# Layer norm in chunks of two tiles with flips amid the matmuls, a convolution spread over the weight gradients, and pinned weight pieces in a fused backward kernel

## The chip, the cores and the metric

The kernel runs on one core of a Trainium2 chip. The metric is the device time of one execution in microseconds (us), lower is better. All inputs and outputs are bfloat16. Executions of one kernel scatter by some 3 to 5 us to either side of their median, so a difference of a few us between two kernels is only told from several runs of both on the same chip, and a difference of 2 us between two single traces is not told at all.

## The reference, cut to what matters

The reference is the forward value and all gradients of a sum of two branches on a layer-normalised input:

```python
xn  = layernorm(x)                                   # x: [2048, 1024]
A   = xn * (causal_conv(shift(k) * v) + D * shift(k) * v)      # long convolution
B   = (relu(xn @ W_gate) * (xn @ W_up)) @ W_down     # W_gate, W_up: [1024, 3584]
out = x + A + B
# returned: out, and the gradients of x, k, v, shift_k, ssm_k, ssm_D, W_gate, W_up, W_down
```

The MLP branch B has the large matrix products. The convolution of branch A is done with transforms written as small matmuls, of which the copies out of PSUM go to ScalarE and VectorE.

## The kernel before

The matrix work of B comes in four phases, and the convolution's steps are woven into the first and second ones:

1. **First phase** (`hidden`): gate, up and hidden gradient, for 2 halves of 8 row tiles and 7 blocks of 512 columns. At its very start the layer norm runs in chunks, and TensorE "flips" (transposes) each normalised tile into `xnT`.
2. **Weight gradients** (`grad_down`, `grad_in`).
3. **Output phase** (`out_phase`): `h @ W_down`, for 16 row tiles. Beside it, the weights of the last phase are loaded transposed.
4. **Last phase** (`grad_x`): the gradient of x, and a tail after the last matmul.

The start and the loop of the first phase (cut):

```python
LN_CHUNKS = (1, 1, 2, 4, 4, 4)
self.e1 = tc.alloc_tile_pool(name="b_e1", bufs=3, side="left")  # ht AND gh live in these 3 buffers
...
def gate_up(sp):
    while len(xT) < sp + 2:                 # flips of both tiles, just before they are used
        while len(self.xn) <= len(xT):
            next(ln)                        # one more chunk of layer norm
        xT.append(self.flip_xn(len(xT)))
    ...
    for s in (sp, sp + 1):                  # up, and the store of h
        self.gemm8(ps, xT[s], wu)
        ht = self.e1_tile("ht")
        ...
        nc.sync.dma_start(out=h_d[...], in_=ht[:])
def grad(sp):
    for s in (sp, sp + 1):
        self.gemm8(ps, gT[s], wd)           # ps_h
        gh = self.e1_tile("gh")
        nc.scalar.copy(out=gh[:], in_=ps[:])
        ...
```

The mixing of the two branches: each piece of MLP work tells its nominal length, and that length times the pace is what the convolution has to wait for its next step. A lower pace makes the convolution slower.

```python
A_START = 55_000                            # ns of MLP work before the convolution starts
yield 0.9, b.hidden(...)
yield 1.3, b.grad_down(...)
yield 1.3, b.grad_in(...)
```

The output phase and the tail (cut):

```python
for st in range(16):
    hT = self.tall(h_d, st, "hT")                             # transposed load, SyncE
    nc.sync.dma_start(out=ya[:], in_=y_d[rows, :])
    nc.sync.dma_start(out=xe[:], in_=xn_d[rows, :])
    nc.sync.dma_start(out=xr[:], in_=x[rows, :])
    if st < 8:                                                # 8 pieces of 256 rows
        nc.sync.dma_start_transpose(out=wT[:, :, c:c + 256], in_=w[c:c + 256, :])
    nc.vector.tensor_tensor(out=ya[:], in0=ya[:], in1=xe[:], op=ALU.mult)
    nc.vector.tensor_tensor(out=ya[:], in0=ya[:], in1=xr[:], op=ALU.add)
    ...                                                       # 56 matmuls; o0 = ps + ya; store o0
# tail of the last phase, per row tile
V.tensor_scalar(out=gm[:], in0=gt[:], scalar1=m[:, 4:5], scalar2=None, op0=ALU.add)
for ob in range(2):
    V.scalar_tensor_tensor(out=gx[:, oc], in0=xn[:, oc], scalar=m[:, 7:8], in1=gx[:, oc], ...)
    V.scalar_tensor_tensor(out=o1[:, oc], in0=gx[:, oc], scalar=rstd, in1=gm[:, oc], ...)
```

The order of instructions on an engine comes from a priority that each instruction gets when it is traced (`pri.now()`, `pri.late()`). `keep_in_program_order` pins an instruction behind what was traced before it on its engine.

## Time and profile before

| | before |
|---|---|
| median of the first three runs | 2003.51 us (1997.66 to 2004.28) |
| profiled execution (span) | 1995.9 us |
| first phase: first matmul of the weight gradients starts at | 712.7 us |
| weight gradients | 688.2 us |
| output phase | 199.5 us |
| last phase | 386.6 us |
| after the start of the last matmul | 8.8 us |

The phases are read from the timeline of TensorE: each begins with the first matmul into its own PSUM tile (`ps_d`, `ps_o`, `ps_x`). Their lengths add up to the span. (The prediction's 8.4 us for the tail counts from the end of the last matmul.) Two of TensorE's waits (engine, line, tile, what it waited for, us in total, times, longest):

```profile
PE ps_g L599 <- DVE xnT L625: 13.0, 4, 7.6
PE ps_o L799 <- DMA hT<-h_d: 5.6, 3, 2.8
```

These are the two that the change is mainly aimed at: 13.0 us for flipped tiles at the start, 5.6 us for `hT` in the output phase.

### The profile page before, as it was taken

To read this page: it belongs to the slowest core of one execution; us is meant where nothing else is said; L and a number is where in the kernel's file an instruction comes from. 1 tells how busy PE (TensorE), PEld (TensorE's weight loads), DVE (VectorE), ACT (ScalarE), POOL (GpSimd) and SP (SyncE) were. 2 spreads that over 40 slices of the span, in tenths; PEclk is the share of its full clock that TensorE was granted. 3 is DMA by queue.
4 is the path that set the end of the run, shared out by engine and by line. 5 is a ranking of instruction groups with operands and counts; after the bars stand their busy time and mean duration, and the time that the engine had idled before them with its cause. 6 is when DMAs were issued, how large, how long until landed. Compare 5 with 4: busy or idle time off the path is not lost.

```text
span 1995.9 us, 27044 instructions
## 1 busy us (share of the span) xinstructions
PE 1929.1 (97%) x10817; PEld 914.2 (46%) x11022; DVE 995.7 (50%) x1460; ACT 693.8 (35%) x912; POOL 15.5 (1%) x36
## 2 busy tenths in 40 slices
PE   5999999999999999999999999999999999999998
PEld 2445445445444444444454444444444444444443
DVE  4879679679677747666685650000122222333322
ACT  5665365456446428484564741111000000000000
POOL 1000000000000000000000000000000000000000
PEclk9999999999999999999999999999999999999999
DMA  9864676974674774444645359432999555445551
GB/s 280 219 167 130 168 190 159 219 191 124 170 184 127 199 208 126 121 136 131 197 145 138 110 157 316 148 97 67 224 264 231 137 124 120 120 119 125 125 125 40
DMA packets 614895, 318.32 MB, mean 159 GB/s; under 512 B 449896, under 2 KB 584048, under 8 KB 614768
## 3 DMA queue, kind: packets, MB, share of 16 engines
q1 hardware_dynamic: 613488, 312.38, 59.7%
q0 software_dynamic: 1280, 4.20, 0.6%
q8 instruction: 86, 1.41, 0.3%
q14 instruction: 41, 0.34, 0.1%
HBM read 141.36 MB, written 95.44 MB: 119 GB/s over the span
## 4 chain that ended last, share of the span: by engine, by line
PE 46%; ACT 2%; SPq 1%; DMA 1%; issue 1%; DVE 0%; DVEq 0%
PE ps_x L832 19%; PE ps_w L715 17%; PE ps_o L799 8%; PE ps L65 1%; SPq L791 1%; DMA hT<-h_d 1%; ACT G L69 1%; ACT H L69 0%; SPq L768 0%; ACT K L69 0%; ACT wi L753 0%; DMA out_dram<-wi 0%; ACT B L69 0%; PE pst L280 0%; SPq L785 0%
## 5 line engine op out<-in xcount | busy, mean ns | idle before, releaser
L715 PE MATMUL ps_w<-ugs,xn_nat 128*128 128x512 bf16 x1746 | 395.3, 379 | 3.3 <-issue 1.0
L599 PEld LDWEIGHTS <-xnT 128*128 128x128 bf16 x1792 | 169.7, 99 | 217.5 <-issue 23.8
L715 PEld LDWEIGHTS <-xn_nat 128*128 128x128 bf16 x1792 | 170.9, 98 | 203.3 <-issue 8.4
L599 PE MATMUL ps_g<-wg,xnT 128*128 128x512 bf16 x869 | 211.3, 388 | 18.9 <-DVE xnT L625 13.0
L715 PE MATMUL ps_d<-g_nat,hs 128*128 128x512 bf16 x867 | 205.1, 381 | 4.4 <-DMA hs<-h_d 2.5
L599 PE MATMUL ps_h<-wdT,goT 128*128 128x512 bf16 x875 | 205.1, 379 | 1.4 <-issue 0.3
L599 PE MATMUL ps_u<-wu,xnT 128*128 128x512 bf16 x868 | 204.2, 379 | 1.5 <-issue 0.3
L799 PE MATMUL ps_o<-wd,hT 128*128 128x512 bf16 x878 | 193.1, 379 | 6.6 <-DMA hT<-h_d 5.6
L832 PE MATMUL ps_x<-wuT,guT 128*128 128x512 bf16 x878 | 197.5, 379 | 1.0
L832 PE MATMUL ps_x<-wgT,ggT 128*128 128x512 bf16 x878 | 197.3, 379 | 0.9
L801 DVE TENSOR_TENSOR o<-ps_o,ya 128x512 bf16<-128x512 f32 x32 | 21.5, 688 | 272.5 <-PE ps_o L799 272.5
L753 ACT CAST wi<-ps_w 128x512 bf16<-128x512 f32 x112 | 65.5, 586 | 233.4 <-PE ps_w L715 225.0
L799 PEld LDWEIGHTS <-hT 128*128 128x128 bf16 x896 | 87.4, 98 | 112.1 <-DMA hT<-h_d 7.1
L832 PEld LDWEIGHTS <-ggT 128*128 128x128 bf16 x896 | 87.7, 98 | 105.7
L832 PEld LDWEIGHTS <-guT 128*128 128x128 bf16 x896 | 87.7, 98 | 105.7
L834 DVE CUSTOM_DVE_ANT_0 gx<-ps_x,gy 128x512 f32<-128x512 f32 x32 | 22.1, 691 | 226.2 <-PE ps_x L832 215.5
L672 ACT CAST gh<-ps_h 128x512 bf16<-128x512 f32 x112 | 65.5, 585 | 190.1 <-PE ps_h L599 108.3
L599 PEld LDWEIGHTS <-goT 128*128 128x128 bf16 x896 | 84.1, 98 | 97.8 <-issue 6.1
L715 PEld LDWEIGHTS <-hs 128*128 128x128 bf16 x896 | 82.7, 98 | 100.7 <-issue 10.0
L291 DVE STREAM_TRANSPOSE flp<-B 128x1024 f32<-128x1024 f32 x48 | 90.2, 1934 | 47.1 <-ACT B L69 46.7
L69 ACT CAST C<-ps 128x1024 bf16<-128x1024 f32 x96 | 96.8, 1017 | 47.4 <-PE ps L65 47.4
L660 DVE SCALAR_TENSOR_TENSOR ru<-ru,ps_u 128x512 bf16<-128x512 bf16 x112 | 76.3, 681 | 71.0 <-PE ps_u L599 55.2
(156 smaller groups left out, 1711.0 us busy)
## 6 DMA issues: line engine op xcount, KB each, us to landing
ug_d<-ru SPq DMA_DIRECT2D x112, 256.0 KB, 3.1
ugs<-ug_d SPq DMA_DIRECT2D x112, 256.0 KB, 4.4
wg<-in_B_W_gate_dram SPq DMA_DIRECT2D x56, 256.0 KB, 5.0
wu<-in_B_W_up_dram SPq DMA_DIRECT2D x56, 256.0 KB, 3.2
h_d<-ht SPq DMA_DIRECT2D x112, 128.0 KB, 1.9
hs<-h_d SPq DMA_DIRECT2D x56, 256.0 KB, 4.4
out_dram<-wi SPq DMA_DIRECT2D x56, 256.0 KB, 2.2
gt<-in_grad_out_dram SPq DMA_DIRECT2D x32, 256.0 KB, 3.9
```

The source lines that it names most:

```text
L65: self.nc.tensor.matmul(out, lhsT=lhsT, rhs=rhs, start=start, stop=stop)
L69: self.nc.scalar.copy(out=out, in_=in_)
L291: self.nc.vector.transpose(out=df[:, c0:c0 + 32, :], in_=sf[:, c0:c0 + 32, :])
L599: self.nc.tensor.matmul(ps[:], lhsT=xT[:, kt * P:(kt + 1) * P], rhs=w(kt), start=(kt == 0), stop=(kt == self.DT - 1))
L660: nc.vector.scalar_tensor_tensor(out=ru[s][:, 1, :], in0=ru[s][:, 0, :], scalar=0.0, in1=ps[:], op0=ALU.is_gt, op1=ALU.mult)
L672: nc.scalar.copy(out=gh[:], in_=ps[:])
L715: self.nc.tensor.matmul(ps[:], lhsT=lhsT(st), rhs=rhs(st), start=(st == 0), stop=(st == self.ST - 1))
L753: nc.scalar.copy(out=wo[:, d, :], in_=ps[:])
L799: nc.tensor.matmul(ps[:], lhsT=hT[:, kt, :], rhs=self.wd[:, kt, oc], start=(kt == 0), stop=(kt == self.FT - 1))
L801: nc.vector.tensor_tensor(out=o0[:, oc], in0=ps[:], in1=ya[:, oc], op=ALU.add)
L832: nc.tensor.matmul(ps[:], lhsT=T[:, kt, :], rhs=W[:, kt, oc], start=(i == 0), stop=(i == n - 1))
L834: V.tensor_tensor_reduce(out=gx[:, oc], in0=ps[:], in1=gy[:, oc], scale=1.0, scalar=0.0, op0=ALU.add, op1=ALU.add, accum_out=m[:, ob:ob + 1])
```

## The change

The intent has four parts. **A**: the flips of later tiles are traced between the matmuls of earlier ones, so that TensorE has work while VectorE copies them, and the layer norm goes in smaller chunks. **B**: the convolution gets pace 1.0 in the weight gradients. **C**: the last phase's weights are loaded in 16 pieces of 128 rows, one per row tile, each pinned. **D**: a step of the tail moves to ScalarE. The diff, cut to its core:

```diff
-    LN_CHUNKS = (1, 1, 2, 4, 4, 4)
+    LN_CHUNKS = (1, 1, 2, 2, 2, 4, 4)
...
+            if i == 2:
+                self.tc.keep_in_program_order(mean)
...
-                    if ahead:
-                        next(ln, None)
...          # in grad(sp):
+                        if ahead and s == sp + 1:
+                            flip(min(sp + 6, HS))
                         ps = self.ps_tile("ps_h")
...          # the first block
                 if ahead:
+                    flip(2)
+                    next(ln)
                     yield from gate_up(0)
+                    next(ln)
+                    yield from gate_up(2)
+                    next(ln)
                 for sp in range(0, HS, 2):
...
                     yield from grad(sp)
+                    if ahead and sp + 4 < HS:
+                        next(ln, None)
+                        yield from gate_up(sp + 4)
...          # output phase
-            if st < 8:
-                w, wT = (Wg, self.wgT) if st < 4 else (Wu, self.wuT)
-                c = (st % 4) * 256
-                nc.sync.dma_start_transpose(out=wT[:, :, c:c + 256], in_=w[c:c + 256, :])
+            w, wT = (Wg, self.wgT) if st < 8 else (Wu, self.wuT)
+            c = (st % 8) * P
+            tc.keep_in_program_order(nc.sync.dma_start_transpose(out=wT[:, :, c:c + P], in_=w[c:c + P, :]))
...          # tail
-            V.tensor_scalar(out=gm[:], in0=gt[:], scalar1=m[:, 4:5], scalar2=None, op0=ALU.add)
-                V.scalar_tensor_tensor(out=gx[:, oc], in0=xn[:, oc], scalar=m[:, 7:8], in1=gx[:, oc], ...)
-                V.scalar_tensor_tensor(out=o1[:, oc], in0=gx[:, oc], scalar=self.rstd[:, st:st + 1], in1=gm[:, oc], ...)
+                nc.scalar.activation(out=w[:, oc], in_=xn[:, oc], func=ACT.Identity, scale=m[:, 5:6], bias=m[:, 4:5])
+                V.scalar_tensor_tensor(out=gx[:, oc], in0=gx[:, oc], scalar=self.rstd[:, st:st + 1], in1=gt[:, oc], ...)
+                V.tensor_tensor(out=o1[:, oc], in0=gx[:, oc], in1=w[:, oc], op=ALU.add)
...          # loads: the third chunk of x goes ahead of the up weights
-        yield 1.3, b.grad_down(g, h_d, out_9)
-        yield 1.3, b.grad_in(xn_d, ug_d, out_7, out_8)
+        yield 1.0, b.grad_down(g, h_d, out_9)
+        yield 1.0, b.grad_in(xn_d, ug_d, out_7, out_8)
```

More of the change, by code (lines that the diff above doesn't have):

```diff
@@ L557, in layer_norm @@
                     self.tc.keep_in_program_order(total)
-            V.tensor_scalar(out=b(0), in0=f(0), scalar1=1.0 / D, scalar2=None, op0=ALU.mult)
+            mean = V.tensor_scalar(out=b(0), in0=f(0), scalar1=1.0 / D, scalar2=None, op0=ALU.mult)
+            if i == 2:
+                self.tc.keep_in_program_order(mean)
             V.tensor_copy(out=f(1), in_=b(0))
@@ L640, in hidden, with flip @@
                 ru, ahead = {}, fb + half == 0
-                def gate_up(sp):
-                    while len(xT) < sp + 2:
+                def flip(n):
+                    while len(xT) < n:
                         while len(self.xn) <= len(xT):
@@ L646, in gate_up @@
                         xT.append(self.flip_xn(len(xT)))
-                    if ahead:
-                        next(ln, None)
+                def gate_up(sp):
+                    flip(sp + 2)
                     for s in (sp, sp + 1):
@@ L684, in hidden @@
                         gT.append(self.load_T(g, s0 + len(gT), "goT"))
-                    if ahead:
-                        if sp + 2 < HS:
-                            yield from gate_up(sp + 2)
-                    else:
+                    if not ahead:
                         yield from gate_up(sp)
                     yield from grad(sp)
+                    if ahead and sp + 4 < HS:
+                        next(ln, None)
+                        yield from gate_up(sp + 4)
                 if ahead:
@@ L824, in grad_x @@
             pr = p_ev.tile([P, D], BF16, name="pr")
+            w = p_ev.tile([P, D], F32, name="w")
             m = p_sm.tile([P, 8], F32, name="m")
@@ L840, in grad_x @@
             V.tensor_scalar(out=m[:, 6:8], in0=m[:, 4:6], scalar1=-1.0 / D, scalar2=None, op0=ALU.mult)
-            V.tensor_scalar(out=m[:, 4:5], in0=m[:, 6:7], scalar1=self.rstd[:, st:st + 1], scalar2=None, op0=ALU.mult)
+            V.tensor_scalar(out=m[:, 4:6], in0=m[:, 6:8], scalar1=self.rstd[:, st:st + 1], scalar2=None, op0=ALU.mult)
             o1 = p_ev.tile([P, D], BF16, name="o1")
-            gm = p_ev.tile([P, D], F32, name="gm")
-            V.tensor_scalar(out=gm[:], in0=gt[:], scalar1=m[:, 4:5], scalar2=None, op0=ALU.add)
             for ob in range(2):
                 oc = slice(ob * 512, ob * 512 + 512)
-                V.scalar_tensor_tensor(out=gx[:, oc], in0=xn[:, oc], scalar=m[:, 7:8], in1=gx[:, oc], op0=ALU.mult,
-                                       op1=ALU.add)
-                V.scalar_tensor_tensor(out=o1[:, oc], in0=gx[:, oc], scalar=self.rstd[:, st:st + 1], in1=gm[:, oc],
+                nc.scalar.activation(out=w[:, oc], in_=xn[:, oc], func=ACT.Identity, scale=m[:, 5:6], bias=m[:, 4:5])
+                V.scalar_tensor_tensor(out=gx[:, oc], in0=gx[:, oc], scalar=self.rstd[:, st:st + 1], in1=gt[:, oc],
                                        op0=ALU.mult, op1=ALU.add)
+                V.tensor_tensor(out=o1[:, oc], in0=gx[:, oc], in1=w[:, oc], op=ALU.add)
                 nc.sync.dma_start(out=out1[rows, oc], in_=o1[:, oc])
@@ L908 @@
     load(1)
-    first = [b.col_block(B_W_gate, 0, "wg"), b.col_block(B_W_up, 0, "wu")]
+    first = [b.col_block(B_W_gate, 0, "wg")]
     load(2)
+    first.append(b.col_block(B_W_up, 0, "wu"))
     load(3)
+    load(4)
     first.append(b.row_block_T(B_W_down, 0, "wdT"))
     goT = [b.load_T(g, i, "goT") for i in range(4)]
-    load(4)
+    load(5)
     a.load_shift()
-    load(5)
+    load(6)
     ln = b.layer_norm(xn_d, a.tmp, "tmp", a.sm)
```

## The prediction

> **What bounds the kernel now.** I read the page first, then a table of busy time by 50 us stretches, then the timeline of TensorE and VectorE at the start, the waits, the SyncE timeline in the output phase, and the tail.
>
> ```profile
> PE 1929.1 (97%) x10817; PEld 914.2 (46%) x11022; DVE 995.7 (50%) x1460; ACT 693.8 (35%) x912; POOL 15.5 (1%) x36
> ```
>
> TensorE is busy 1929.1 of 1995.9 us. None of the matmuls goes away in this change, so all there is to gain is the 66.8 us in which TensorE idles, plus the time in which it runs slowly. Where is the idle time? By stretches (columns: time, busy us of TensorE, weight loads, VectorE, ScalarE, GpSimd, granted clock, DMA share, GB/s):
>
> ```profile
> 0.00:22.00 22.00, 2.32 (x17) 1.67 (x18) 10.52 (x50) 10.84 (x21) 5.80 (x16) 1.00 0.98 274
> 47.00:63.00 16.00, 13.51 (x66) 6.30 (x67) 10.15 (x30) 12.54 (x26) 2.20 (x4) 0.89 0.90 207
> 712.00:850.00 138.00, 131.02 (x871) 63.95 (x886) 79.83 (x84) 70.98 (x86) 0.41 (x1) 0.99 0.53 151
> 850.00:1000.00 150.00, 146.48 (x963) 71.02 (x978) 94.67 (x91) 95.50 (x113) 0.41 (x1) 1.00 0.55 155
> 1000.00:1195.00 195.00, 190.98 (x1315) 95.73 (x1337) 130.23 (x141) 108.97 (x132) 0.41 (x1) 1.00 0.47 136
> 1195.00:1401.00 206.00, 205.00 (x938) 93.39 (x955) 1.24 (x3) 34.55 (x59) 0.00 (x0) 1.00 0.49 154
> 1440.00:1504.00 64.00, 58.13 (x264) 25.97 (x268) 10.34 (x16) 0.00 (x0) 0.00 (x0) 1.00 1.16 258
> ```
>
> So: about 20 us at the start, 14.5 us in the weight gradients while the convolution runs beside them (712 to 1195), against only 1.0 us in 206 us once it is done, 5.9 us in the output phase at 1440 to 1504, and a tail of some 8 us after the last matmul. The four parts of the change aim at these four places.
>
> **The start**, TensorE's timeline (start, us, engine, line, what, count, idle before and its releaser):
>
> ```profile
> 13.07 1.04 PE L623 MATMUL pst_x<-ident,ln_x 128*128 128x128 bf16 x8 [1.72 <-DVE ln_x L580]
> 21.75 6.43 PE L599 MATMUL ps_g<-wg,xnT 128*128 128x512 bf16 x16 [7.63 <-DVE xnT L625]
> 33.31 3.40 PE L599 MATMUL ps_g<-wg,xnT 128*128 128x512 bf16 x15 [0.79 <-DVE xnT L625]
> 46.76 5.31 PE L599 MATMUL ps_g<-wg,xnT 128*128 128x512 bf16 x15 [2.24 <-DVE xnT L625]
> 62.25 3.63 PE L599 MATMUL ps_g<-wg,xnT 128*128 128x512 bf16 x15 [2.38 <-DVE xnT L625]
> ```
>
> The second flip is through TensorE at 14.1, yet its copy runs on VectorE only at 21.0, behind the whole layer norm of the third chunk:
>
> ```profile
> 20.20 0.88 DVE L580 TENSOR_SCALAR ln_x<-ln_x,rstd 128x1024 bf16<-128x1024 bf16 x2
> 21.00 1.28 DVE L625 COPY xnT<-pst_x 128x1024 bf16<-128x1024 bf16 x2
> ```
>
> It is an order problem, not a busy engine. The later three waits are the flips themselves: two transposes back to back, two copies (0.68 us each), and no matmul that doesn't need them in between.
>
> **The output phase**: SyncE issues in order, and its queue is full (start, us, engine, line, what):
>
> ```profile
> 1482.94 3.52 SPq L768 DMA_TRANSPOSE hT<-h_d  x1
> 1488.55 8.67 SPq L791 DMA_TRANSPOSE wuT<-in_B_W_up_dram  x1
> 1497.32 4.36 SPq L768 DMA_TRANSPOSE hT<-h_d  x1
> ```
>
> From one hT issue to the next it is 14.4 us (1482.94 to 1497.32), while TensorE eats an hT in 56 matmuls of 0.2158 us (49 of them in 10.74 us, with the gap 10.79 for 50), 12.1 us. The store of three tiles ahead is used up at 1474, and three waits of 0.65, 2.16 and 2.80 us follow, all named "DMA hT<-h_d".
>
> **What the Trainium skill says.** (1) "TensorE: Matmul & The Clock Gate", Part 1: TensorE starts at half clock, is released after some 3.4 us of sustained work and falls back after an idle window. The trace agrees: from 21.75 to 28.02 sixteen matmuls take 6.27 us (0.39 each) against 3.45 warm, a loss of 2.8; and the flips and idle from 43.5 to 46.76 are followed by sixteen in 5.15 us, 1.7 too many, in the stretch with clock 0.89. So a wait costs more than its length. (2) "Perfetto Trace Analysis", What "DMA-bound" means: one of the bounds is the issuing engine's sequencer, whose track is then solid DMA slices. SyncE's between 1440 and 1504 is, as quoted. (3) "DMA: Bandwidth & Descriptors", Issuing engines are not separate DMA queues: all transfers share the same 16 engines. That matters for the third rival below: the DMA share is 1.16 in that stretch and 0.48 in the last phase.
>
> **The change part by part.**
>
> Part A, layer norm and flips. Chunk 2's mean is pinned behind the second copy, its input is loaded ahead of the up weights, the 4-tile chunk that held tiles 4 to 7 becomes two of 2, and from grad on the flips stand between the two ps_h groups. The first GEMM needs the gate weights (four issues at 1.7 to 3.6 us, at most 7.4 us to landing, so 11) and a copy, which can follow the second flip at 14.1: first GEMM at about 14.3 instead of 21.75, **7.4 us**. The half-clock loss of 2.8 stays, only earlier. Tiles 2 and 3: mean at about 14.9 (before 14.55), and the chain then takes as before (14.55 to 21.08), so they are normalised at 21.4; gate and up of tiles 0 and 1 last until about 14.3 + 6.3 + 3.45 = 24, so the flips don't wait for them and the old 0.79 us stays. Tiles 4 and 5: in a 2-tile chunk with a chain of about 6.5 us plus sums; they are flipped 1.7 us into grad(0), and the copies (2 x 0.68) lie beside the second ps_h group (1.73 us). So the waits of 2.24 and 2.38 go, **4.6 us**, and with them the 1.7 us of half clock: **1.7**. I take off 1.7 for VectorE's new order (0.7 us copies against the multiplications with gh). Sum **12**.
>
> Part B, pace 1.3 to 1.0 in the weight gradients. The code's nominal lengths make the convolution 8 x 119 = 952 us. The first phase has 336 yields x 1.73 x 0.9 = 523, less 55 of start: 468 used. The remaining 484 need 484 / 1.3 / 1.73 = 215 of the 336 yields now, and 280 after. So it ends about 56 yields, 97 us, before the weight gradients do, instead of 206 us. That leaves room for the 7 MB of down weights, which then load (1200 to 1250 moved 326 GB/s, so some 23 us). What is gained: at 750 to 780 ScalarE is at 9.6 to 9.9 of 10 and matmuls wait for its evictions; in the first phase, at pace 0.9, TensorE has no wait of this kind at all. Excess idle in 712 to 1195 is 14.5 less 483 x 1.0 / 206 = 2.3, so 12.2; of it 2.5 is the slab from h_d, which stays; the waits named for the convolution's matmuls add up to 6.4. I take **5**.
>
> Part C, weights of the last phase in 16 pieces of 128 rows. Same bytes; a piece of half the size should take SyncE about what an hT of the same shape takes, 3.5 to 4.4 us in place of 7.1 to 8.7. A round of the queue is then 14.4 - 4.2 = 10.2 us, under TensorE's 12.1. The last up piece goes out with tile 15 at about 1570 on the old clock, before the last phase needs it (1606 and later). Excess idle was 5.9 less 0.4; I take **5**.
>
> Part D, the tail. Now the VectorE steps from 1987.47 to 1992.86 take 5.39 us. The gm over 1024 elements (0.66 apart from the next) goes; ScalarE makes w (about 0.6 for 512 elements, as CAST of the same shape, 0.586) beside a VectorE step that waits for nothing of m; four VectorE steps of 0.7 stay, of which one can be early. **1 us**; all tiles but the last hide it.
>
> Sum 12 + 5 + 5 + 1 = 23. From 2003.5: 1980.5. As runs lie at either 1998 or 2004, I say **1980**.
>
> **Rivals.**
> 1. *The start is bound by something else next*: DMA runs at 0.98 to 1.09 of its share in the first 47 us and the transposed wdT and goT hold SyncE from 7.19 to 26.42. TensorE comes to ps_h at 32.6 rather than 40.0. For it: landing takes 5.7 us, so the last goT is there at 32. Against: the first is needed first and lands at about 27. It would cost up to 5 us: 1985.
> 2. *Stalls only move*: the convolution's waits are its own chains (evict, flip, next matmul), spread over more rounds, and the same sum comes back. For it: 1.0 of the waits is on the flip by VectorE. Against: the first phase, where pace 0.9 shows none. It would make part B nothing: 1985. If the flips' copies also still end the wait, 1990.
> 3. *The pieces keep DMA full through the whole output phase*: two 128-row transposes and four 256 KB transfers per 12.1 us, what the last phase moves in 24.2 us at share 0.48, so about 0.96. For it: hT issues take up to 4.97 us when the share is over 1. Against: 1.16 was borne. Then part C gives 0 to 2: 1984.
> 4. *Better than I think*: all of the 12.2 us in part B, and the first GEMM before the second flip (12.2 us): 1970.
>
> **Range and chances.** One rival coming true costs 3 to 5 us, two make 1988; the best case is about 1970, and the runs scatter by 6. Range 1969 to 1990. 2% is 40 us, more than the whole idle time that the change can reach (12.7 + 12.2 + 5.5 + 1 = 31): faster by 2% only 0.03, slower 0.01, within 2% 0.96.
>
> **What would show it.** First gate matmul at 14 to 15 us and no wait over 1 us for xnT after it (A). ScalarE no longer full after the switch of phases, the convolution's end near 1290, and idle in the weight gradients down by 5 (B). No wait of ps_o for hT, and SyncE rounds near 10 us (C). 7.4 us instead of 8.4 after the last matmul (D). I am wrong if the first GEMM still starts after 18, if ps_h waits for goT or wdT, or if matmuls of the last phase wait for wuT.

## The result, and the profile after

The changed kernel takes 1992.78 us (median of 4 runs, 1991.63 to 1996.35), against 2001.1 us for the kernel before in the same rounds (4 runs). The ratio of the two is 0.9962, with a 95% interval from 0.9938 to 0.9986. The "within 2%" was right; the time was outside the range of 1969 to 1990. About 8 us came of the 23 that were added up; and these were taken off 2003.5, the median of the first three runs, where the four runs give 2001.1.

The phases of the two traces show where:

| us | before | after | gain | predicted |
|---|---|---|---|---|
| first phase | 712.7 | 715.9 | −3.2 | +12 (A) |
| weight gradients | 688.2 | 681.1 | +7.1 | +5 (B) |
| output phase | 199.5 | 199.4 | +0.1 | +5 (C) |
| last phase | 386.6 | 386.6 | 0 | 0 |
| after the start of the last matmul | 8.8 | 8.4 | +0.4 | +1 (D) |

One part gave more than was expected of it, one nothing, and the largest turned into a loss. (The loss of 3 us is no accident of two traces: it is there in the means of ten, below.) The page's first line and four stretches of the changed kernel (columns as in the prediction):

```profile
PE 1939.9 (97%) x11022; PEld 913.4 (46%) x11022; DVE 987.9 (50%) x1457; ACT 719.7 (36%) x945; POOL 15.5 (1%) x36
```

```profile
0.00:22.00 22.00, 9.23 (x44) 4.68 (x45) 10.79 (x51) 13.41 (x26) 4.88 (x15) 1.00 0.98 263
716.00:850.00 134.00, 128.60 (x800) 61.20 (x797) 64.36 (x71) 66.61 (x82) 0.41 (x1) 0.99 0.49 146
1000.00:1195.00 195.00, 194.97 (x1235) 93.29 (x1233) 102.64 (x98) 100.90 (x123) 0.41 (x1) 1.00 0.48 136
1440.00:1504.00 64.00, 64.00 (x298) 29.04 (x297) 11.25 (x18) 0.00 (x0) 0.00 (x0) 1.00 0.93 214
```

In the first 22 us TensorE is now busy for 9.23 instead of 2.32 us, so the start did move. In the weight gradients the idle time is almost gone after 1000 us. In the output phase the stretch that had 5.9 us of idle is full. The busy sums of the two pages must not be subtracted: the trace of before lacks 205 of the 11022 matmul records. The phase lengths don't depend on such records, which is why they are used.

**Where the head start of part A went.** First three lines of TensorE's timeline in the kernel before, then the same in the kernel after:

```profile
76.08 3.62 PE L599 MATMUL ps_g<-wg,xnT 128*128 128x512 bf16 x16
...
102.97 0.39 PE L65 MATMUL ps<-hT,R 64*128 64x512 bf16 x2
...
124.03 3.62 PE L599 MATMUL ps_g<-wg,xnT 128*128 128x512 bf16 x16
```

```profile
14.63 5.13 PE L601 MATMUL ps_g<-wg,xnT 128*128 128x512 bf16 x16
...
25.52 3.63 PE L601 MATMUL ps_g<-wg,xnT 128*128 128x512 bf16 x16 [1.41 <-DVE xnT L627]
...
44.47 5.54 PE L601 MATMUL ps_g<-wg,xnT 128*128 128x512 bf16 x16 [7.52 <-ACT gh L677]
49.85 3.62 PE L601 MATMUL ps_u<-wu,xnT 128*128 128x512 bf16 x16
...
72.10 3.62 PE L601 MATMUL ps_g<-wg,xnT 128*128 128x512 bf16 x16
...
102.37 0.39 PE L65 MATMUL ps<-hT,R 64*128 64x512 bf16 x2 [3.14 <-DVE hT L77]
102.69 3.31 PE L601 MATMUL ps_g<-wg,xnT 128*128 128x512 bf16 x8
105.93 0.60 PE L65 MATMUL ps<-hT,R 64*128 64x512 bf16 x2
...
127.21 3.62 PE L601 MATMUL ps_g<-wg,xnT 128*128 128x512 bf16 x16
```

Read the same piece of work in both. The first gate matmul is 7.1 us ahead (14.63 against 21.75, which the prediction shows). The gate of the second block, after all eight tiles of the first, is 4.0 us ahead (72.10 against 76.08). The large terms are these: 7.1, plus the waits of 2.24 and 2.38 us and the 1.7 us of half clock that went, less a new wait of 7.52 us and the slow matmuls after it (sixteen from 44.47 to 49.85, 5.38 us against 3.45, so 1.9), is 4.0. Smaller ones cancel: the first sixteen matmuls take 4.97 us instead of 6.27, so 1.3 of the 2.8 us of half clock went too, while the wait for the third tile grew from 0.79 to 1.41 and 0.47 us for `goT` and small gaps came in. Then several waits of 0.2 to 0.8 us take 2.3 (the convolution's first matmul on `ident` starts at 95.23 against 96.89, 1.7 ahead). At the convolution's second step on `hT` the changed kernel is 3.0 us behind (105.93 against 102.97): it waited 3.14 us, and the eight matmuls after that took 3.24 instead of 1.73 us. It is 3.2 behind at the gate of the third block, and at the end of the phase.

**What the 7.52 us are.** SyncE's timeline of the kernel after (start, us it is held, line, what):

```profile
20.47 7.15 SPq L618 DMA_TRANSPOSE goT<-in_grad_out_dram  x4
...
29.46 4.75 SPq L594 DMA_DIRECT2D wg<-in_B_W_gate_dram  x3
34.32 0.40 SPq L666 DMA_DIRECT2D h_d<-ht  x1
```

and VectorE's and ScalarE's:

```profile
41.07 0.43 DVE L665 TENSOR_TENSOR ht<-ru 128x512 bf16<-128x512 bf16 x1 [7.14 <-DMA h_d<-ht]
...
43.84 0.59 ACT L677 CAST gh<-ps_h 128x512 bf16<-128x512 f32 x1 [8.61 <-DMA h_d<-ht]
```

The first `ht` is ready near 23 us, as the up matmuls start at 19.6. Its store is issued at 34.32, since SyncE is in the middle of eight transposed loads and then of three weight loads; it lands just before 41.07. Until then the buffer is not free, and three buffers serve both `ht` and `gh`. So VectorE stands 7.14 us before the fourth of them, ScalarE 8.61 us before the `gh`, and TensorE, which needs the PSUM tile that this `gh` empties, 7.52 us. In the kernel before, SyncE's queue was just as full at that time, with the first store at 32.19, but nothing was ready earlier. The head start of 7.1 us moved the data forward and not the store.

**The output phase.** One round of SyncE in the kernel after, and the largest wait of its queue in that phase:

```profile
1481.42 3.96 SPq L778 DMA_TRANSPOSE hT<-h_d  x1
...
1486.05 0.42 SPq L793 DMA_DIRECT2D ya<-y_d  x1
1489.69 0.33 SPq L795 DMA_DIRECT2D xe<-xn_d  x1
...
1490.80 5.53 SPq L800 DMA_TRANSPOSE wuT<-in_B_W_up_dram  x1
1496.42 3.56 SPq L778 DMA_TRANSPOSE hT<-h_d  x1
```

```profile
SPq L795 <- DVE ya L801: 34.0, 11, 3.1
```

From one `hT` to the next it is 15.0 us here, 13.6 on average, against the 12.1 us in which TensorE eats one. Between 1486.47 and 1489.69 SyncE issues nothing: it stands before the load of `xe`, whose buffer is freed by VectorE's product of two tiles before, and that product can't run until the `ya` just issued has landed. This happens 11 times, 3.1 us each. The two waits of TensorE for `hT` that result are 2.42 us at 1556.81 and 1.47 us at 1584.31; they stand later than those of before.

**The tail.** One group line of the page, and VectorE's last step:

```profile
L855 ACT ACTIVATE w<-xn,m 128x512 f32<-128x512 bf16 x32 | 24.3, 806 | 565.5 <-issue 317.2
```

```profile
1986.95 1.40 DVE L858 TENSOR_TENSOR o<-gx,w 128x512 bf16<-128x512 f32 x2 [0.93 <-ACT w L855]
```

ScalarE's step takes 806 ns, and VectorE waits 0.93 us for the first of the two. One step of VectorE, `gx` on line 856, runs from 1984.93 to 1985.67: ahead of the last two small steps of `m`, for which ScalarE waits, and not beside ScalarE.

### The profile page after: what moved, and what is told of

It reads as the page before. It is cut to its first block, busy times and chain, and to the rows that moved or that the text cites. A ratio compares the mean times of both kernels' runs of the same rounds, so it can differ in the third digit from the quotient of the medians. Undisturbed runs are those within 1.5% of the kernel's fastest.

```text
span 1991.3 us, 27328 instructions
## 1 busy us (share of the span) xinstructions
PE 1939.9 (97%) x11022; PEld 913.4 (46%) x11022; DVE 987.9 (50%) x1457; ACT 719.7 (36%) x945; POOL 15.5 (1%) x36
## 3 DMA queue, kind: packets, MB, share of 16 engines
q8 instruction: 86, 1.41, 0.3%
## 4 chain that ended last, share of the span: by engine, by line
PE 58%; issue 2%; DMA 1%; SPq 0%; ACT 0%; DVE 0%
PE ps_w L725 19%; PE ps_x L842 18%; PE ps_o L808 9%; PE ps_d L725 8%; PE ps L65 4%; DMA hT<-h_d 1%; PE pst L280 0%; SPq L800 0%; DMA xn_nat<-xn_d 0%; ACT H L69 0%; DVE o L858 0%; ACT B L69 0%; ACT w L855 0%; DVE ya L802 0%; DVE ya L801 0%
## 5 line engine op out<-in xcount | busy, mean ns | idle before, releaser
L725 PE MATMUL ps_w<-ugs,xn_nat 128*128 128x512 bf16 x1792 | 405.5, 379 | 1.3 <-DMA xn_nat<-xn_d 1.3
L725 PEld LDWEIGHTS <-xn_nat 128*128 128x128 bf16 x1792 | 168.7, 98 | 199.3 <-issue 10.4
L855 ACT ACTIVATE w<-xn,m 128x512 f32<-128x512 bf16 x32 | 24.3, 806 | 565.5 <-issue 317.2
L601 PE MATMUL ps_g<-wg,xnT 128*128 128x512 bf16 x896 | 212.7, 386 | 14.3 <-ACT gh L677 7.5
L763 ACT CAST wi<-ps_w 128x512 bf16<-128x512 f32 x112 | 65.4, 586 | 202.1 <-PE ps_w L725 196.4
L291 DVE STREAM_TRANSPOSE flp<-C 128x1024 f32<-128x1024 f32 x48 | 89.8, 1928 | 51.5 <-ACT C L69 51.5
```

Source lines behind the costliest of these rows:

```text
L291: self.nc.vector.transpose(out=df[:, c0:c0 + 32, :], in_=sf[:, c0:c0 + 32, :])
L601: self.nc.tensor.matmul(ps[:], lhsT=xT[:, kt * P:(kt + 1) * P], rhs=w(kt), start=(kt == 0), stop=(kt == self.DT - 1))
L725: self.nc.tensor.matmul(ps[:], lhsT=lhsT(st), rhs=rhs(st), start=(st == 0), stop=(st == self.ST - 1))
L763: nc.scalar.copy(out=wo[:, d, :], in_=ps[:])
L855: nc.scalar.activation(out=w[:, oc], in_=xn[:, oc], func=ACT.Identity, scale=m[:, 5:6], bias=m[:, 4:5])
```

## The experiments

Seventeen kernels were run, all with results equal to the reference within its tolerance. Kernels ran beside the kernel before (11 runs of it each time, medians of 2000.06 to 2002.55 us). The changed kernel itself ran only in the first call, so a comparison with it goes over the ratios of two calls, or over traces. Its interval, 0.9938 to 0.9986, is wide: by times alone xr_acc, pool_loads, start63, undo_c and xe3 are not told from it. The theory was: A's gain is lost to the late stores of `h_d`, B works as meant, C's queue is held by loads that wait for each other. The rivals are those of the prediction, of which the most important were "transposed loads bound the start" and "DMA is full in the output phase".

**only_a**: the kernel before with part A alone.

> The kernel before with part A alone (layer norm chunks, pinned mean, flips amid the matmuls). If part A's early start is given back because stores of h_d sit in SyncE's queue behind the transposed loads, the first gate matmul comes at about 14.6 us as in the changed kernel, the wait of about 7.5 us near 37 to 44 us is there again, and the first phase ends later than before by about 3 us: 2004 against 2001, ratio 1.000 to 1.003. If the loss came from an interplay with parts B to D, part A alone gains 5 to 12 us: ratio 0.994 to 0.9975.

Measured: 2002.09 us (1998.46 to 2005.82), ratio 1.000 [0.9985, 1.0016]. The wait for `gh` is 7.4 us, the one for the convolution's `hT` 3.1 us. Part A alone is worth nothing that can be told, and it brings both new waits by itself.

**pace1**: the kernel before with part B alone.

```diff
-        yield 1.3, b.grad_down(g, h_d, out_9)
-        yield 1.3, b.grad_in(xn_d, ug_d, out_7, out_8)
+        yield 1.0, b.grad_down(g, h_d, out_9)
+        yield 1.0, b.grad_in(xn_d, ug_d, out_7, out_8)
```

> The kernel before with part B alone (pace 1.0 in the two weight gradients). By the milestones of the two traces the weight gradients took 688.3 us before and 681.1 after. If spreading the convolution removes the waits on its evictions, this run gains 7 to 9 us (ratio 0.9955 to 0.9965), with no wait of the convolution's matmuls on ScalarE over 0.5 us. Rival: the stalls only move, gain 0 to 2 us.

Measured: 1994.38 us, ratio 0.9963 [0.9947, 0.9979], weight gradients 680.3 us (before 688.2). The pair of numbers alone gives what the whole change gives (0.9962).

**pool_store**: the changed kernel, with the stores of `h_d` in the first two blocks issued by GpSimd, that is on a queue where no transposed load is ahead of them.

```diff
-                        nc.sync.dma_start(out=h_d[(s0 + s) * P:(s0 + s + 1) * P, cols], in_=ht[:])
+                        eng = nc.gpsimd if half == 0 and fb < 2 else nc.sync
+                        eng.dma_start(out=h_d[(s0 + s) * P:(s0 + s + 1) * P, cols], in_=ht[:])
```

> The changed kernel with the stores of h_d of the first two blocks of the first half issued by GpSimd in place of SyncE, 16 stores in all. Theory: they are late because SyncE's queue is taken by transposed loads, so the three small buffers stay full, ScalarE and VectorE stop, then TensorE. Then the wait of 7.5 us on gh and the one of 3.1 us on hT are gone and the cold restarts with them: 10 to 15 us less than the changed kernel, about 1980. Rival: the 16 DMA engines are full (share 1.13 at 33 to 47 us) and a store lands late whoever issues it: 0 to 4 us less.

Measured: 1986.3 us (1985.74 to 1989.29), ratio 0.9923 [0.9909, 0.9938]. Two lines of TensorE's timeline:

```profile
36.82 3.62 PE L601 MATMUL ps_g<-wg,xnT 128*128 128x512 bf16 x16
...
61.29 1.90 PE L601 MATMUL ps_h<-wdT,goT 128*128 128x512 bf16 x7 [2.76 <-DMA goT<-in_grad_out_dram]
```

The gate that started at 44.47 after a stall starts at 36.82 without any. So the late store was the cause of that stall. The rival, that a store lands late whoever issues it, is refuted: from GpSimd the first goes out at 23.4 us, and stores there land within 3.6 to 6.2 us. The waits of 0.2 to 0.8 us between 76 and 88 us are gone as well. The gain was 7 us rather than the 10 to 15 expected. Part of it met the next limit: three waits for `goT`, 4.6 us in all, which is the prediction's first rival come true once the stores were out of its way. And the wait for the convolution's `hT`, which was expected to go, stayed with 2.44 us and half clock after it, so the late stores are not its main cause.

**before_pool_store**: the same edit in the kernel before, as a control.

> Control: the same move of the 16 stores to GpSimd in the kernel before. There TensorE reaches these stores some 7 us later and has no wait on them, so by the queue theory nothing changes: within 2 us of before. If the move itself helps whatever the start does, it gains as much here as in the changed kernel, 10 us or more.

Measured: 2001.91 us, ratio 0.9995 [0.9981, 1.0009]. Nothing, as expected: the late stores cost time only where their data is ready early.

**undo_c**: the changed kernel with the old eight unpinned pieces.

> The changed kernel with the last phase's weights loaded as before, 256 rows with each of the first eight tiles and not pinned. The output phase took 199.5 us before and 199.3 after, so part C should be worth nothing: within 1.5 us of the changed kernel. If the pieces were worth the 5 us that I predicted and something else hid it, this run is 4 to 6 us slower than the changed kernel.

Measured: 1993.85 us (1990.84 to 2001.16), ratio 0.9968 [0.9951, 0.9985], output phase 200.6 us. Part C as a whole is worth nothing that can be told.

**no_pin**: the changed kernel with the 16 pieces, not pinned.

```diff
-            tc.keep_in_program_order(nc.sync.dma_start_transpose(out=wT[:, :, c:c + P], in_=w[c:c + P, :]))
+            nc.sync.dma_start_transpose(out=wT[:, :, c:c + P], in_=w[c:c + P, :])
```

> The changed kernel with the sixteen pieces not pinned in SyncE's order. If the pin is what puts a piece behind the blocked loads, the scheduler will issue pieces earlier and the waits for hT change place or go: 0 to 5 us less. If the pin keeps pieces from crowding out hT, the waits for hT grow: 2 to 6 us more.

Measured: 1999.97 us, ratio 0.9992 [0.9978, 1.0006], output phase 205.4 us with 8.0 us of waits for `hT`. Small pieces without the pin are worse than the large ones; with the pin they are equal.

**xr_acc**: the changed kernel, with the sum held in another tile, so that the buffers come free in another order.

```diff
-            nc.vector.tensor_tensor(out=ya[:], in0=ya[:], in1=xe[:], op=ALU.mult)
-            nc.vector.tensor_tensor(out=ya[:], in0=ya[:], in1=xr[:], op=ALU.add)
+            nc.vector.tensor_tensor(out=xe[:], in0=ya[:], in1=xe[:], op=ALU.mult)
+            nc.vector.tensor_tensor(out=xr[:], in0=xe[:], in1=xr[:], op=ALU.add)
...
-                nc.vector.tensor_tensor(out=o0[:, oc], in0=ps[:], in1=ya[:, oc], op=ALU.add)
+                nc.vector.tensor_tensor(out=o0[:, oc], in0=ps[:], in1=xr[:, oc], op=ALU.add)
```

> The changed kernel with the elementwise sum of the output phase held in xr in place of ya, so that ya and xe come free at once and no load in SyncE's queue waits for the landing of another. Theory: the queue's round of 13 to 15 us holds a wait of about 3.1 us for ya to land; without it a round is about 10.5 us, under TensorE's 12.1, and both waits for hT (2.42 and 1.47 us) and the cold restart are gone: 4 to 5 us less than the changed kernel. Rival: the DMA engines are full at a share of 0.95, the round stays over 13 us and nothing is gained.

Measured: 1989.1 us (1987.94 to 1990.96), ratio 0.994 [0.9927, 0.9952]; output phase 193.4 us, no wait for `hT`. The gain came as expected, but not in the way expected. SyncE's largest wait in that phase:

```profile
SPq L793 <- DVE xe L801: 30.6, 10, 3.1
```

The wait only moved from `xe` to `ya`, and a round is still about 13.5 us. What helped, as far as the trace shows, was the order that the scheduler found: two pieces of weights instead of four ahead of the fourth `hT` (issued at 1411.3 instead of 1416.8), and the last two pieces after the last `hT`. So more tiles were in store, and they lasted to the end. By times, too, this run is told from undo_c only just (0.9927 to 0.9952 against 0.9951 to 0.9985). It doesn't show that the wait costs the time; it only shows that the phase can be done in 193.4 us, which is its 16 x 56 matmuls at 0.2158 us.

**pool_xr**: both edits, pool_store and xr_acc.

> The changed kernel with both mends, stores of h_d of the first two blocks by GpSimd and the sum held in xr. If both causes hold and don't touch each other, their gains add: 14 to 20 us less than the changed kernel, 1973 to 1979, which would be what the change was meant to give. If one wait only hides another, the gain is no more than the larger of the two alone.

Measured: 1980.17 us (1978.19 to 1981.73), ratio 0.9893 [0.988, 0.9907]. The two add up within the scatter, to less than the 14 to 20 us expected, as each gave less.

**before_xr**: the edit of xr_acc in the kernel before.

> The kernel before with the sum held in xr, as a control: there a piece of 256 rows and an hT alone take 12 us or more of SyncE, so a round stays over 14 us whatever the sum does and the output phase stays at 199 to 200 us: within 1.5 us of before. If it gains 5 us here too, the pieces of part C were not needed for the gain in the changed kernel.

Measured: 1998.18 us (1993.87 to 2003.81), ratio 0.9983 [0.9963, 1.0003], output phase 195.6 us. The time can't be told from none, but the trace gained 3.9 us in the phase where none was expected, and five other traces with the large pieces and the old sum have 199.2 to 200.6. A miss: the order of loads matters with large pieces too.

**px_got, px_start, px_both**: pool_xr with `goT` asked for one step earlier; pool_xr with the convolution started later; both.

```diff
-                    while len(gT) < min(sp + 2, HS):
+                    while len(gT) < min(sp + (4 if ahead else 2), HS):      # px_got, px_both
...
-A_START = 55_000
+A_START = 63_000                                                            # px_start, px_both
```

> The kernel with both mends, and the fifth and sixth transposed goT asked for one grad earlier, so that they go ahead of some of the convolution's first loads in SyncE's queue. In the kernel with both mends ps_h waits 3.6 us for goT at 55 to 61 us, as rival 1 of the prediction said. If the queue's order is the cause, these waits shrink by 2 to 4 us and the kernel by about 2 to 4 us: 1976 to 1978. If the transfer engines are full and only that counts, nothing changes.

> The kernel with both mends, and the convolution's start 8 us of nominal work later (63 in place of 55). In every kernel with part A TensorE waits 1.8 to 3.1 us for the copy of hT, which stands on VectorE behind the tables. If VectorE's tables are the bound there, a later first step takes that wait and its half clock away, 2 to 4 us: 1976 to 1978. Rival: it is the convolution's own first load or the transposes that come late, and the wait stays or moves.

> Both of the two together: 4 to 7 us less than the kernel with both mends if the two waits are apart, 1973 to 1976. If the first wait feeds the second, only the larger of the gains is left.

Measured: 1980.82 us (0.9895), **1975.9 us** (1972.76 to 1978.95, ratio 0.9873 [0.985, 0.9897]) and 1978.2 us (0.988). Asking for `goT` earlier is a miss. In px_got one wait of 6.0 us stands where those for `goT` had been (put down to an early step of the layer norm, which had long been done) and 2.0 us for `wdT`; in px_both it is 5.9 us for `goT` and 3.5 for `wdT`. What comes last there is not settled. Starting the convolution 8 us of nominal work later left waits of 0.7 us for the convolution's `hT` in place of 3.14. It also shortened the weight gradients to 676.7 us, with the wait for `hs` at the switch of phases gone; why that went too is not settled. px_start has the lowest median of all the kernels here.

**start63**: the later start alone, in the changed kernel.

> The changed kernel with the convolution's start 8 us of nominal work later and nothing else. If the wait for hT at 99 to 102 us (3.14 us, then half clock) is VectorE still at its tables, it is gone, and the first phase is 4 to 5 us shorter; the stall of 7.5 us at 37 to 44 us stays. If the gain of the last round came from the stores by GpSimd alone, nothing changes here.

Measured: 1989.32 us (1986.16 to 1991.37), ratio 0.9937 [0.9924, 0.995]; first phase 712.7 us (3.2 less than the changed kernel), weight gradients 676.6 us. The wait goes as expected, and the stall behind the stores stays, with 7.1 us; the first phase gains a little less than the 4 to 5 us expected, and the 4.5 us in the weight gradients were not expected at all.

**xe3, ps_xe3**: three buffers for `xe` and `xr` and one for `o0` in the output phase (SBUF has no room for more), in the changed kernel, and in it with pool_store and the later start.

> The changed kernel with three buffers for xe and for xr and one for o0 (2 KB more in all, which just fits). In the changed kernel and also in the one with the sum in xr, SyncE waits 3.1 us in each round for a 256 KB load to land and be multiplied. With a third buffer that wait should be gone: rounds of hT at 12.1 us, set by TensorE, not 13.6, no wait of ps_o for hT, the output phase 193.5 us in place of 199.4, some 5 us less than the changed kernel. Rival: the transfer engines (share 0.95) set the round; then it stays near 13.6 and the phase near 199.

> The changed kernel with stores by GpSimd, the later start of the convolution and the third buffers, in place of the sum in xr: if the third buffer mends the output phase as well as the sum in xr does, this equals the fastest kernel so far (ratio 0.9873 to before, about 1976), within 3 us.

Measured: 1994.31 us (0.9969) and 1980.93 us (1979.77 to 1988.47, 0.9904), output phases 201.6 and 202.5 us. Both missed. With a third buffer SyncE stood before the same load, 9 times and 27.8 us, now for `ya`; and the single `o0` brought a new wait of TensorE, 7.2 us in 5 times. The edit changed two things, so it says nothing on the cause.

**pool_loads**: the changed kernel with the three plain loads of each tile issued by GpSimd. Same bytes, same buffers, and the same waits of one load for another, but not in SyncE's queue. If it is the transfers that set the round, this can't help.

```diff
-            nc.sync.dma_start(out=ya[:], in_=y_d[rows, :])
+            nc.gpsimd.dma_start(out=ya[:], in_=y_d[rows, :])
...          # and so for xe and xr
```

> The changed kernel with the output phase's three elementwise loads (ya, xe, xr) issued by GpSimd in place of SyncE; the bytes are the same. Run xe3 missed: the wait for a landing stayed in SyncE's queue, so it didn't test what it was for. Here no load that waits stands in SyncE's queue. If the queue's waits made the round, hT goes out every 12.1 us, paced by TensorE, no wait of ps_o for hT, the output phase is 193.5 us in place of 199.4, and the kernel 5 to 6 us shorter than the changed one. Rival: the transfer engines, at 0.95, make it; then hT still goes out every 13 us or more and the phase stays over 198.

Measured: 1987.32 us (1984.05 to 1991.27), ratio 0.9935 [0.9919, 0.9951]; output phase 193.4 us. SyncE's timeline (two stretches), the use of the engines in one stretch, and the queue's largest wait:

```profile
1433.41 3.62 SPq L778 DMA_TRANSPOSE hT<-h_d  x1
...
1445.50 3.56 SPq L778 DMA_TRANSPOSE hT<-h_d  x1
...
1546.25 5.77 SPq L778 DMA_TRANSPOSE hT<-h_d  x1
...
1552.70 7.72 SPq L800 DMA_TRANSPOSE wuT<-in_B_W_up_dram  x1
1560.52 4.77 SPq L778 DMA_TRANSPOSE hT<-h_d  x1
```

```profile
1500.00:1550.00 50.00, 49.74 (x229) 22.62 (x233) 10.33 (x16) 0.00 (x0) 6.55 (x12) 1.00 1.22 222
```

```profile
SPq L778 <- PE ps_o L808: 37.6, 13, 7.0
```

Up to 1494 us the rounds are 12.1 us, TensorE's own pace, and SyncE waits for TensorE to free an `hT`, 37.6 us in all. So a queue without the waiting loads is fast enough there, and with the same bytes the phase as a whole runs at TensorE's pace. But this is not a clean test of the wait. The scheduler again found another order: three pieces instead of four ahead of the fourth `hT`, which is issued at 1411.85 instead of 1416.79, and this lead of 4.9 us is by itself more than TensorE's two waits, 3.9 us together. And the last five rounds are 13.3 us on average without any wait of SyncE: there the transposed loads hold it for 4.4 to 7.8 us. The DMA share is then 1.22, and an `hT` lands after 8.9 us in the median of the phase instead of 5.7. So in these rounds it is the transfers that seem to set the pace, and the tiles in store keep TensorE fed.

**ps_loads**: pool_store, the later start and pool_loads together.

> Stores of h_d by GpSimd in the first two blocks, the convolution's start at 63, and the three loads by GpSimd: if pool_loads mends the output phase, this equals the fastest kernel so far, ratio 0.987 to before, 1972 to 1977 us. If GpSimd's loads bring a cost of their own, 1978 or more.

Measured: 1976.57 us (1974.22 to 1977.7), ratio 0.9878 [0.9863, 0.9893]: the same as px_start within the scatter.

The phases of the traces, in us. Single first phases scatter. The seven traces with the changed first phase and nothing mended in it (after, only_a, undo_c, xr_acc, no_pin, xe3, pool_loads) run from 714.0 to 719.5, mean 716.7; the three with the old one (before, pace1, before_xr) from 712.7 to 714.9, mean 713.6. The stall behind the stores, 6.8 to 9.1 us, is in all of the seven and in none of the three. With the stores moved and the later start, the three traces have 706.0, 707.3 and 713.3 (ps_xe3, one of its two longest executions, with one wait of 5.4 us for `goT`).

| | first | weight gradients | output | last | tail |
|---|---|---|---|---|---|
| after | 715.9 | 681.1 | 199.4 | 386.6 | 8.4 |
| only_a | 717.4 | 687.6 | 199.2 | 386.6 | 8.8 |
| pace1 | 714.9 | 680.3 | 199.3 | 386.6 | 8.8 |
| pool_store | 708.5 | 682.0 | 202.1 | 386.6 | 8.4 |
| pool_loads | 714.0 | 682.9 | 193.4 | 386.6 | 8.4 |
| start63 | 712.7 | 676.6 | 200.1 | 386.6 | 8.4 |
| px_start | 706.0 | 676.7 | 193.4 | 386.6 | 8.4 |

## Why the prediction was right or wrong

**Part A, the first step, was right.** The first GEMM starts at 14.63, predicted at 14.3, and no flip is waited for by more than 1.41 us from the third tile on (the prediction's own sign was 1 us).

**Part A, the sum of 12, is the step that failed most.** It took the gains at the start as gains of the end. What TensorE met next was not a busy engine but three buffers, held by stores that stood in SyncE's queue behind the transposes. That cost 9.4 us with the half clock after it. The prediction looked at this very queue, in the first rival ("the transposed wdT and goT hold SyncE from 7.19 to 26.42"), but asked only when the transposed loads land, not what else must pass the queue after them. That rival in its own form, `ps_h` waiting for `goT`, was only 0.5 us in the changed kernel, and 4.6 us once the stores were mended (pool_store). The second loss, some 2.3 us of small waits for `gh` and `ru`, is in part the same stores again: ScalarE stands 5.66 us behind one until 75.90. The third, 3.14 us with 1.5 us of half clock, is the convolution's first transposed tile: the copy of `hT` runs on VectorE at 101.10 us, against 99.09 before. VectorE is busy 19.93 of the 20 us from 80 to 100 with the convolution's tables, as it is in the kernel before; and the late store just named stops it for 3.28 us at 76.52. That the later start takes this wait away is shown (start63); how much of the lateness each of the two makes is not shown, but 2.44 us of the wait are left in pool_store, where these stores are not late. The order of causes is shown: only_a has the stall and the wait for `hT`, the kernel before has neither, and pool_store removes the first.

**Part B was right in its mechanism and too small.** Predicted 5, measured 7.1 (7.9 in pace1). The waits for the convolution's evictions and flips between 712 and 1195 us fell from 6.4 to 1.6 us, and ScalarE is busy 27.26 of the 30 us from 750 to 780 instead of 29.33. Against these 4.8 us the waits for the loads `hs` and `xn_nat` grew by 2.1; the rest of the gain stands under no name in the waits, and its cause is open. The convolution's last store moved from 1214.6 to 1300.2 us, predicted near 1290. The second rival, that the stalls would only move, is refuted.

**Part C was wrong at the step "A round of the queue is then 14.4 - 4.2 = 10.2 us".** It was 13.6. The pieces do hold SyncE for less, 3.85 to 5.56 us, so their saving is there in part. Missing is the term of 3.1 us in which SyncE stands before the load of `xe`: without it the round would be 10.5. In the kernel before, a round with a piece had no such wait: `ya` was issued at 1488.08, ahead of the 256-row piece and the `hT`, had all of their 13 us to land, and `xe` followed at 1501.72 without a pause. The wait stood there as well (16.5 us in 5 times), but in the rounds without a piece. So a part of the large piece's time was wait that it hid, and halving the piece laid it bare: the two are not to be subtracted from each other. The sum of a round was built from the lengths of issues, as if a queue had no waits of its own. The third rival said the transfers would keep the gain to 0 to 2 us. For the phase as a whole pool_loads refutes it, with 193.4 us for the same bytes, but its last five rounds come near it. (The rival's own line is misread: the issue of 4.97 us, at 1530.32, lies where the share is 0.82, not over 1.) That the wait alone costs the 6 us between 199.4 and 193.4 is not shown, since every edit that won them also changed the order of the loads. undo_c and no_pin show that C as it is gives nothing that can be told, and that the pin saves it from costing some 6 us (205.4 against 199.4 in the phase).

**Part D** was predicted at 1 and gave 0.4. The overlap failed first: the `gx` step that was to run beside ScalarE stands ahead of the last two steps of `m` instead, so `m` and ScalarE come later by about 0.5 us. This is an estimate: in the kernel before, these steps of `m` start 0.20 us apart, here 0.74. And the ScalarE step was taken as a CAST of 586 ns, and it is an activation with scale and bias read from SBUF, at 806 ns, another 0.2. The Trainium skill would have told: "ScalarE: Activation LUTs", What ACT_TABLE_LOAD costs, gives 186 ns + 0.833 ns per element for an activation with immediate scale and bias, and some 93 ns for each operand that is a pointer. For 512 elements and two pointers this is an estimate of 799 ns, and the trace agrees with it.

**The chances** were sound: within 2% had 0.96. The range was too narrow at its upper end, because the rivals were each priced at 3 to 5 us and a lost part A was not among them. A gain of that size does exist, made up otherwise: with the stores moved, the sum in another tile and the convolution started later, px_start is at 1975.9 us, below the prediction. Its trace has 6.7 us of the 12 in the first phase, 11.5 in the weight gradients in place of 5, and 6.1 in the output phase in place of 5. It beats the kernel before by 1.3% and the changed kernel by some 0.9% (0.9873 over 0.9962).

**What stays open.** In px_start, waits of 4.4 us for `goT` at 55 to 65 us remain, and those of some 4 to 6 us for VectorE's `ru` in the first phase, which all kernels have. The `goT` waits couldn't be mended by asking earlier (px_got). A fourth buffer for `ht` and `gh` would test the buffers apart from the queue, but it doesn't fit into SBUF. For part C, the changed kernel's order of loads with only the wait taken out has not been run.

## What to carry to other kernels

When a change makes data ready earlier, follow that data to where its buffer is freed: a store that stands in an in-order queue behind loads can hand the whole head start back, as 7.1 us became a stall of 7.5 here. Build the round of an issuing engine from its issues and from its waits; if a load in it needs a buffer that another load of the same queue must first help to free, try the waiting loads on another engine's queue, and look whether the transfers then set the pace. Test each part of a change by itself and by phase: here two changed numbers did all the work, and the larger edits were worth nothing until one more line was mended.

## What the Trainium skill lacked or had wrong

- "DMA: Bandwidth & Descriptors", Issuing engines are not separate DMA queues, says that issuing from several engines saves only the time on the sequencer, "which is usually small relative to the DMA itself". The saving was large: 16 stores moved to GpSimd took away a stall of 7.5 us (pool_store). With three plain loads per tile moved there and the same bytes, the output phase came to 193.4 us from 199.4 (pool_loads), though the order of the loads changed with them. The section doesn't say that a DMA which waits or is issued slowly holds all those behind it on the same engine.
- The same page, Latency and other measured facts, gives 261 GB/s for a transposed load with a non-contiguous middle dimension, but no time for which a load of such a size holds the engine that issues it. Here 128 rows of 3584 columns held SyncE for 3.6 to 5.6 us in the changed kernel and up to 7.8 in pool_loads, where the DMA share was 1.22, and 256 rows for 7.1 to 8.7 us.
- "Perfetto Trace Analysis", What "DMA-bound" means, names a solid sequencer track as the sign of a queue that bounds. In the changed kernel's output phase the track had a hole of some 3.1 us in each of 11 rounds, and a round of the queue, 13.6 us, was still longer than TensorE's 12.1. Its section DMA Optimizations advises to balance DMAs over engines where the issuing engine looks busy with slices; here (pool_loads, with the order changed too) it went with a gain of 6.0 us where that engine stood waiting.
- "TensorE: Matmul & The Clock Gate", Part 1, has the fall to half clock after an idle window of some 3.4 us. Here a wait of 3.14 us was enough: the eight matmuls after it took 3.24 instead of 1.73 us. So a wait below that length can cost its length and half as much again. The length alone doesn't decide: in pool_store the matmuls after a wait of 2.44 us were slow (eight in 3.12 us), those after one of 2.76 us were not.
